# The second product's last part in 128x64 tiles of the array: two matmuls for 64 tokens each in place of one for 128

## The chip, the cores and the metric

The kernel runs on one core of a Trainium2 chip. Its engines are TensorE (PE in the profile, PEld its weight loads), VectorE (DVE), ScalarE (ACT), GpSimd (POOL) and SyncE (SP), which run side by side and wait for each other by semaphores. The metric is device time in microseconds (us) of one execution; the median over several runs counts.

## The reference

Two steps follow each other: an attention with a window of 32 positions and 32 global tokens per batch, and a two-layer product with a gate between the layers. The change lies in the last line.

```python
# attention, B=8 batches, H=8 heads, 512 local + 32 global tokens, head_dim 64
out_g = softmax(scale * q_g @ [k_g, k_l].T) @ [v_g, v_l]
out_l = softmax([scale * q_l @ k_g.T, masked(scale * q_l @ k_l.T)]) @ [v_g, v_l]   # |i - j| <= 32
x = concat(out_g, out_l).transpose(0, 2, 1, 3).reshape(B * S, H * D)                # 4352 x 512
# two products, w_in 512 x 2048, w_out 2048 x 512
h = x @ w_in
g = h * clip(h + 3, 0, 6) / 6
return g @ w_out                                                                    # 4352 x 512
```

## The kernel before

The work is cut by batch. For each of the eight batches the local attention is done in four steps of 128 queries (`local_step`), the 32 global queries in one (`global_steps`), and then the two products are done for the 512 local tokens (`moe_local`). The global tokens of all batches, 8 x 32 = 256, are kept until the end and get their two products there (`moe_global`).

A local step has these matmuls. L741 multiplies 128 queries with the global keys, on the whole 128x128 array. L748 does the window: for each pair of heads and each group of 32 queries a matmul with 64 rows of the array and 32 of its columns, so that eight such 64x32 tiles fit on the array (two halves of rows for two heads, four quarters of columns for four groups of queries). L797 (early batches) turns the probabilities, and L830 (L822 for batch 0) multiplies them with the values. L822 uses slices of 64, 32 and 96 rows of the array beside whole ones. For the global queries L865 computes the scores, again on 64x32 tiles, the first eight matmuls with 32 columns of moving data and the next eight with 512; L904 turns the probabilities and L918 multiplies them with the values.

The products: `first` computes 128 of the 2048 inner columns for 512 tokens (L941, four matmuls that add up over the 512 model columns), ScalarE applies the gate's first half (L948), VectorE the second (L952), and the result goes in half precision to the tile `gs`, with the inner columns on the partitions. `second` computes 128 tokens of the output: 16 matmuls (L964) add up over the 2048 inner columns in one PSUM tile `m`; the weights loaded into the array are 128x128 of `gs` (128 inner columns by 128 tokens) and the moving data are 512 columns of `w_out`. The 16 are issued in four steps of four (`q`). ScalarE or VectorE then copies `m` to `ot` (L410 or L412) and SyncE stores it (L981). For the last 128 tokens of the last batch the output is made in two halves of 256 columns (`halves=2`). There are three tiles `m` and two tiles `gs`.

The order of the work is not written out by hand. Every step is handed to a planner with `add(engine, duration, ...)`, its dependencies, a due time (`key`, shifted by a table of ranks) and the buffers that it takes and gives back. The planner simulates the engines with these durations, sorts all steps by the start that it finds, and the program issues them in that order, each engine its own. Each step of four matmuls in `second` has a duration of 865 ns there and 8 instructions. The ranks move the second products of batches 6 and 7 towards the end: they run from 266.8 us on, among the last attention steps and first products, and the last 112 matmuls of L964, with nothing else between them, end the work of TensorE. At the start, matmuls on a tile of zeros (L1093) keep TensorE busy while the first data come.

Of the kernel before, what the change touches and what calls it, by code (L numbers as in the profile page):

```python
# [175 lines left out]
class Plan:  # L176
# [16 lines left out]
    def add(self, eng, dur, emit, deps=(), key=0.0, acq=None, rel=(), dma=None, cols=0, ins=0):  # L193

        o = Op(eng, dur, emit, deps, key + RANKS.get(self.at, 0.0), acq, rel, 0, dma)
        o.at, o.cols, o.ins = self.at, cols, ins
        o.can = {eng: dur} if isinstance(eng, str) else dict(zip(eng, dur))
        o.n = len(self.ops)
        self.ops.append(o)
        for r in rel:  # L200
            r.held += 1
        return o
# [120 lines left out]
def kernel(  # L323
# [12 lines left out]
    nc = tc.nc  # L336
    P = 128

    B, H, Sl, D = q_l.shape
# [4 lines left out]
    NJ = Sl // P  # L344
    NDFF = dff // P
# [20 lines left out]
    def many(n, shape, dtype, name, pool=sb):  # L366
        return [pool.tile(shape, dtype, tag=f"{name}{i}", name=f"{name}{i}") for i in range(n)]
# [5 lines left out]
    psM = many(3, [P, 512], FP32, "m", pp)  # L373
# [19 lines left out]
    gs = many(2, [P, NDFF, 512], FP16, "gs")  # L393
# [3 lines left out]
    w_out_t = sb.tile([P, NDFF, dm], FP16, tag="wout", name="wout")  # L397
# [10 lines left out]
    def copy(op, out, in_):  # L408
        if op.eng == "ACT":
            nc.scalar.copy(out=out, in_=in_)  # L410
        else:
            nc.vector.tensor_copy(out=out, in_=in_)  # L412
# [521 lines left out]
    def first(c, n, t0, x, xdeps, xrel, set_, key):  # L934

        k = 512 // n

        def pe(op):
            for i in range(k):
                for m in range(NP):  # L940
                    nc.tensor.matmul(out=psM[op.slot][:, i * n:(i + 1) * n],  # L941
                                     lhsT=w_in_t[:, m, (c + i) * P:(c + i + 1) * P],
                                     rhs=x()[:, m, t0:t0 + n], start=(m == 0), stop=(m == NP - 1))
        f = add("PE", 865 + 10 * (k - 1), pe, list(xdeps) + [*wi[c // 4], set_], key=key, acq="M", rel=xrel, cols=2048, ins=2 * k * NP)
        to = add("ACT", 0, lambda op: None, [f], key=key - 2, acq="t1")

        def re(op):
            nc.scalar.activation(out=t1[to.slot], in_=psM[f.slot], func=RELU, bias=0.5, scale=1.0 / 6.0)  # L948
        a = add("ACT", 477, re, [to], key=key - 2)

        def st_(op):
            nc.vector.scalar_tensor_tensor(out=gs[set_.slot][:, c:c + k, t0:t0 + n],  # L952
                                           in0=t1[to.slot].rearrange("f (k t) -> f k t", k=k), scalar=1.0,
                                           in1=psM[f.slot].rearrange("f (k t) -> f k t", k=k),
                                           op0=ALU.min, op1=ALU.mult)
        return add("DVE", 600, st_, [a], key=key - 1, rel=[f, to])

    def second(t0, gdone, set_, dests, keys, halves=1):
        f, n = None, dm // halves
        for a in range(halves):  # L960
            for q in range(4):
                def pe(op, q=q, a=a):
                    for c in range(q * 4, q * 4 + 4):
                        nc.tensor.matmul(out=psM[(f or op).slot][:, a * n:(a + 1) * n], lhsT=gs[set_.slot][:, c, t0:t0 + P],  # L964
                                         rhs=w_out_t[:, c, a * n:(a + 1) * n], start=(c == 0), stop=(c == NDFF - 1))
                deps = gdone[q * 4:q * 4 + 4] + [wo[q * 4]]
                if f is None:
                    f = s = add("PE", 865 / halves, pe, deps, key=keys[q], acq="M", cols=2048 / halves, ins=8)
                else:
                    s = add("PE", 865 / halves, pe, deps + [s], key=keys[q] + 0.01 * a,  # L970
                            rel=[set_] if q == 3 and a == halves - 1 else [], cols=2048 / halves, ins=8)
            if a == 0:
                oo = add("DVE", 0, lambda op: None, [s], key=keys[3] - 1, acq="ot")

            def ev(op, a=a):
                copy(op, ot[oo.slot][:, a * n:(a + 1) * n], psM[f.slot][:, a * n:(a + 1) * n])
            c = add(BOTH, (482 / halves, 603 / halves), ev, [s, oo], key=keys[3] - 1, rel=[f])

            for k, (dst, lo, hi) in enumerate(dests):
                def sto(op, dst=dst, lo=lo, hi=hi, a=a):  # L980
                    nc.sync.dma_start(out=dst[:, a * n:(a + 1) * n], in_=ot[oo.slot][lo:hi, a * n:(a + 1) * n])  # L981
                add("SP", 600, sto, [c], key=keys[3] + 0.001 * (k + 4 * a), rel=[oo],
                    dma=(hi - lo, STORE[0] / halves, STORE[1]))

    def moe_local(b, at, span):
        plan.at = None
        set_ = add("ACT", 0, lambda op: None, xdone[b, 0], key=at - 1, acq="gs")
        parts = PART.get(b, (Sl,))
        left = [0]

        def key():
            left[0] += 1
            return at + span * left[0] / 32
        done = []
        for part, n in enumerate(parts):
            t0, k = sum(parts[:part]), 512 // n
            js = range(t0 // P, (t0 + n) // P)
            now = []
            for c in range(0, NDFF, k):
                plan.at = "first", b, part, c // 4  # L1000
                o = first(c, n, t0, lambda: xt[xt_op[b].slot], [d for j in js for d in xdone[b, j]], [xt_op[b]], set_, key())
                now += [o] * k
            done += [now] * len(js)
        for j in range(NJ):
            row = b * S + G + j * P
            plan.at = "second", b, j
            second(j * P, done[j], set_, [(out[row:row + P, :], 0, P)], [key() for _ in range(4)],
                   2 if b == B - 1 and j == NJ - 1 else 1)

    def moe_global(at, span):  # L1010
        deps = [xgd[b] for b in range(B)]
        plan.at = None
        set_ = add("ACT", 0, lambda op: None, deps, key=at - 1, acq="gs")
        k = 512 // (B * G)
        done = [None] * NDFF
        for c in range(0, NDFF, k):
            plan.at = "first", B, c // 4
            done[c:c + k] = [first(c, B * G, 0, lambda: xg, deps, [], set_, at + span * c / 24)] * k
        rows = out.rearrange("(b s) d -> b s d", s=S)
        per = P // G  # L1020
        for i in range(B // per):
            plan.at = "second", B, i
            second(i * P, done, set_, [(rows[i * per + k, 0:G, :], k * G, (k + 1) * G) for k in range(per)],
                   [at + span * (16 + 4 * i + q) / 24 for q in range(4)])

# [2 lines left out]
    for b in range(B):  # L1030
        if b == 0:
            seq = ["q0", "h", "q1", "k", "v0", "v1", "q2", "v2", "q3", "v3", "v4", "i0", "i1", "i2", "i3", "g"]
            for n, what in enumerate(seq):
                k, i, key = what[0], int(what[1:] or 0), -8.0 + 0.05 * n
# [51 lines left out]
        for j in range(NJ):  # L1086
            xdone[b, j] = local_step(b, j, lead + j)
        xgd[b] = global_steps(b, lead + 3.6)
        moe_local(b, 4.0 * b + 0.5, 4.0)
    moe_global(4.0 * b + 2.5, 1.5)  # L1090

    spare = {"A": [x[:, 0, :] for x in psA], "M": psM, "S": [x[:, 0, :] for x in psS]}
    order = plan.fill(plan.lay(av_last[NEAR, 0]), lambda ring, i: lambda: nc.tensor.matmul(  # L1093
        out=spare[ring][i], lhsT=idle[:, 0:P], rhs=idle))
# [36 lines left out]
```

## Time and profile before

| | us |
|---|---|
| median of 3 runs (lowest to highest) | 330.35 (330.26 to 330.73) |
| the profiled execution, its own time | 330.47 |
| its span in the profile | 328.7 |
| busy: PE, DVE, ACT, POOL | 317.9, 264.4, 249.1, 105.6 |
| L964, 560 matmuls and 560 weight loads: busy | 128.4 and 51.2 |
| L964 from 266 us on: 144 matmuls of 512 columns, 32 of 256 | 33.5 and 4.6 |

Mean durations in the groups by line: a 512-column matmul of L964 379 ns, a 256-column one 273 ns, a weight load 98 ns. The granted clock of TensorE was 0.995 of full speed over the span.

[...] Matmuls follow each other in a pipeline, so that one of 379 ns can start every 216 ns; the distance between the starts, not the duration, says what a matmul costs in a stream. The chain of waits goes back from the last instruction to what released it, step by step; in order of time its rows say where the end was made. In a row of a timeline, the size behind the operation (128*128, 64*32) is the rows and columns of the array that the instruction uses, and the size after it the moving data.

### The profile page before, as it was taken

Reading aid. Unit: us, or ns where it says so; the run is one execution under the profiler, and the core shown is the slowest. Engines: PE = TensorE matmul, PEld = TensorE weight load, DVE = VectorE, ACT = ScalarE, POOL = GpSimd, SP = SyncE. Lnnn points to the kernel's source line nnn. Section 1 sums busy time; section 2 is a strip of 40 time slices with the busy share of each in tenths; the row PEclk is TensorE's granted clock in tenths of the full one; section 3 lists DMA queues with packets and bytes.
Section 4 is the critical chain, followed back from the end, with each engine's and each line's share of the span. In section 5 each row is a group of like instructions: output and inputs, shape, how many; then the busy total and the mean of one; then the engine's idle time right before and its main releaser. Section 6 shows DMA issues by size and latency. Waiting matters only on the chain.

```text
span 328.7 us, 10251 instructions
## 1 busy us (share of the span) xinstructions
PE 317.9 (97%) x3892; PEld 190.7 (58%) x3892; DVE 264.4 (80%) x972; ACT 249.1 (76%) x787; POOL 105.6 (32%) x139
## 2 busy tenths in 40 slices
PE   8799899999999999999899999999999999999996
PEld 4478795678676555645445545554545545448453
DVE  6999999889979999898899799576987997377100
ACT  4789899879968889886888798587977894466121
POOL 8849626962870962137600500041000000000000
PEclk9979999999999999999999999999999999999999
DMA  9999999999999999399999999969753313100032
GB/s 161 174 190 171 197 281 176 159 200 235 194 155 245 178 206 203 47 136 190 205 191 253 165 224 201 198 106 183 185 130 98 35 27 103 59 7 0 3 97 96
DMA packets 152898, 49.83 MB, mean 152 GB/s; under 512 B 137936, under 2 KB 145936, under 8 KB 152848
## 3 DMA queue, kind: packets, MB, share of 16 engines
q0 software_dynamic: 106560, 17.05, 69.9%
q1 hardware_dynamic: 46288, 32.12, 42.5%
q8 instruction: 30, 0.49, 0.6%
q14 instruction: 20, 0.16, 0.1%
HBM read 35.19 MB, written 8.91 MB: 134 GB/s over the span
## 4 chain that ended last, share of the span: by engine, by line
PE 79%; DVE 10%; DMA 5%; ACT 3%; issue 1%; SPq 0%; ACTq 0%
PE m L964 34%; PE m L941 30%; PE a L830 4%; DVE sm L763 3%; DMA et<-pn 2%; PE s L748 2%; DVE gs L952 2%; PE t L797 2%; DMA st<-ve 2%; ACT sm L774 2%; PE a L822 1%; PE t L677 1%; PE s L741 1%; DMA st<-in_q_l_dram 1%; DVE pn L789 1%
## 5 line engine op out<-in xcount | busy, mean ns | idle before, releaser
L964 PE MATMUL m<-wout,gs 128*128 128x512 f16 (+1 forms) x560 | 128.4, 373 | 0.0
L941 PE MATMUL m<-xt,win 128*128 128x512 f16 (+2 forms) x704 | 120.1, 321 | 1.2 <-DVE gs L952 0.7
L774 ACT ACTIVATE sm<-sm,stat 128x128 f32<-128x128 f32 x256 | 100.0, 393 | 13.9 <-DVE stat L763 13.3
L952 DVE SCALAR_TENSOR_TENSOR gs<-t,m 128x512 f16<-128x512 f32 x136 | 91.0, 683 | 14.6 <-ACT t L948 13.9
L941 PEld LDWEIGHTS <-win 128*128 128x128 f16 x768 | 68.3, 98 | 47.9 <-issue 2.8
L948 ACT ACTIVATE t<-m 128x512 f32<-128x512 f32 x136 | 80.1, 594 | 19.8 <-PE m L941 18.9
L964 PEld LDWEIGHTS <-gs 128*128 128x128 f16 x560 | 51.2, 98 | 50.8 <-issue 1.1
L763 DVE CUSTOM_DVE_ANT_0 sm<-s,mask 128x128 f32<-128x128 f32 x256 | 60.0, 283 | 3.9 <-PE s L748 3.4
L774 ACT ACTIVATION_READ_ACCUMULATOR sm<-sm,stat 128x1 f32 x256 | 48.8, 191 | 0.0
L505 POOL DMA_DIRECT2D ve<-in_v_l_dram x40 | 32.7, 828 | 43.3 <-PE a L918 32.4
L789 DVE TENSOR_TENSOR pn<-sm,stat 128x512 f16<-128x512 f32 x64 | 44.0, 688 | 1.1
L410 ACT CAST xt<-a 64x512 f16<-64x512 f32 x55 | 31.7, 577 | 15.9 <-PE a L830 14.1
L505 POOL DMA_DIRECT2D nat<-in_q_l_dram x30 | 27.5, 916 | 30.6 <-PE t L677 15.1
L505 POOL DMA_DIRECT2D nat<-in_k_l_dram x30 | 27.4, 913 | 8.7 <-DMA wout<-in_moe_w_out_dram 5.3
L410 ACT COPY ot<-m 128x512 f32<-128x512 f32 (+1 forms) x21 | 11.8, 562 | 19.3 <-PE m L964 19.1
L763 DVE DVE_READ_ACCUMULATOR2_ANT stat<- 128x1 f32 x256 | 21.0, 82 | 0.0
L830 PEld LDWEIGHTS <-st 128*128 128x128 f16 x448 | 16.6, 98 | 6.4 <-issue 1.8
L830 PE MATMUL a<-et,st 128*128 128x64 f16 x448 | 17.7, 193 | 1.6 <-DMA et<-pn 1.6
L505 POOL DMA_DIRECT2D ve<-in_v_g_dram x8 | 4.9, 608 | 30.3 <-PE a L918 30.3
L785 DVE RECIPROCAL stat<-stat 128x4 f32<-128x4 f32 x64 | 10.9, 172 | 3.5 <-ACT sm L774 2.9
L412 DVE COPY ot<-m 128x512 f32<-128x512 f32 x14 | 9.6, 686 | 5.0 <-PE m L964 5.0
L741 PEld LDWEIGHTS <-qk 128*128 128x128 f16 x224 | 9.4, 96 | 4.9 <-issue 0.4
(86 smaller groups left out, 274.3 us busy)
## 6 DMA issues: line engine op xcount, KB each, us to landing
out_dram<-ot SPq DMA_DIRECT2D x31, 256.0 KB, 3.7
st<-ve SPq DMA_DIRECT2D x14, 384.0 KB, 8.2
nat<-in_q_l_dram POOLq DMA_DIRECT2D x30, 128.0 KB, 6.3
nat<-in_k_l_dram POOLq DMA_DIRECT2D x30, 128.0 KB, 6.5
st<-ve SPq DMA_DIRECT2D x7, 512.0 KB, 8.6
st<-ve SPq DMA_DIRECT2D x14, 256.0 KB, 7.6
ve<-in_v_l_dram POOLq DMA_DIRECT2D x24, 128.0 KB, 5.9
win<-in_moe_w_in_dram POOLq DMA_DIRECT2D x4, 512.0 KB, 9.6
```

The source lines that it names most:

```text
L410: nc.scalar.copy(out=out, in_=in_)
L505: nc.gpsimd.dma_start(out=dst(op), in_=src)
L741: nc.tensor.matmul(out=ps[:, e, p * P:p * P + G], lhsT=lhs, rhs=kgz[r][:, p, e, :])
L763: nc.vector.tensor_tensor_reduce(out=sm[sm_op.slot][:, h, :], in0=psS[s.slot][:, e, p * P:(p + 1) * P], in1=m, scale=-scale, scalar=3.0e38 ...
L774: nc.scalar.activation(out=sm[sm_op.slot][:, h, :], in_=sm[sm_op.slot][:, h, :], func=EXP, scale=-1.0, bias=stat[stat_op.slot][:, 0, h:h + 1],
L785: nc.vector.reciprocal(out=stat[stat_op.slot][:, 2, h0:h1], in_=stat[stat_op.slot][:, 1, h0:h1])
L789: (nc.gpsimd if op.eng == "POOL" else nc.vector).tensor_tensor(out=pn[pn_op.slot][:, h0:h1, :], in0=sm[sm_op.slot][:, h0:h1, :], in1=stat[ ...
L830: nc.tensor.matmul(out=ps[:, p // 2, c0:c0 + 64], lhsT=st[r][:, u * NJ + j, p * P:(p + 1) * P], rhs=et[et_op.slot][:, 2 * p:2 * p + 2, u * ...
L941: nc.tensor.matmul(out=psM[op.slot][:, i * n:(i + 1) * n], lhsT=w_in_t[:, m, (c + i) * P:(c + i + 1) * P], rhs=x()[:, m, t0:t0 + n], start ...
L948: nc.scalar.activation(out=t1[to.slot], in_=psM[f.slot], func=RELU, bias=0.5, scale=1.0 / 6.0)
L952: nc.vector.scalar_tensor_tensor(out=gs[set_.slot][:, c:c + k, t0:t0 + n], in0=t1[to.slot].rearrange("f (k t) -> f k t", k=k), scalar=1.0, ...
L964: nc.tensor.matmul(out=psM[(f or op).slot][:, a * n:(a + 1) * n], lhsT=gs[set_.slot][:, c, t0:t0 + P], rhs=w_out_t[:, c, a * n:(a + 1) * n ...
```

## The change

`second` gets a parameter `rows_`, the number of tokens per matmul. It is 128 as before for batches 0 to 5, and 64 for the last two batches and the global tokens. With 64, each matmul becomes two: one with the weights of tokens 0 to 63 that writes partitions 0 to 63 of `m`, and one with the weights of tokens 64 to 127 that writes partitions 64 to 127. Both use all 128 rows of the array and 64 of its columns, and both take the same moving data. Each matmul has its own weight load, so there are two of these as well. The durations and instruction counts that are handed to the planner stay as they were.

```diff
-    def second(t0, gdone, set_, dests, keys, halves=1):
+    def second(t0, gdone, set_, dests, keys, halves=1, rows_=P):
...
                     for c in range(q * 4, q * 4 + 4):
-                        nc.tensor.matmul(out=psM[(f or op).slot][:, a * n:(a + 1) * n], lhsT=gs[set_.slot][:, c, t0:t0 + P],
-                                         rhs=w_out_t[:, c, a * n:(a + 1) * n], start=(c == 0), stop=(c == NDFF - 1))
+                        for m in range(0, P, rows_):
+                            nc.tensor.matmul(out=psM[(f or op).slot][m:m + rows_, a * n:(a + 1) * n],
+                                             lhsT=gs[set_.slot][:, c, t0 + m:t0 + m + rows_],
+                                             rhs=w_out_t[:, c, a * n:(a + 1) * n], start=(c == 0), stop=(c == NDFF - 1))
...
             second(j * P, done[j], set_, [(out[row:row + P, :], 0, P)], [key() for _ in range(4)],
-                   2 if b == B - 1 and j == NJ - 1 else 1)
+                   2 if b == B - 1 and j == NJ - 1 else 1, P // 2 if b >= B - 2 else P)
...
             second(i * P, done, set_, [(rows[i * per + k, 0:G, :], k * G, (k + 1) * G) for k in range(per)],
-                   [at + span * (16 + 4 * i + q) / 24 for q in range(4)])
+                   [at + span * (16 + 4 * i + q) / 24 for q in range(4)], 1, P // 2)
```

## The prediction

> **What bounds the kernel now.** I read the page's busy times and its chain of waits first, then the chain in order of time for the part where the change acts, then the timeline of TensorE (PE) there.
>
> ```profile
> span 328.7 us, 10251 instructions
> ...
> PE 317.9 (97%) x3892; PEld 190.7 (58%) x3892; DVE 264.4 (80%) x972; ACT 249.1 (76%) x787; POOL 105.6 (32%) x139
> ...
> PE 79%; DVE 10%; DMA 5%; ACT 3%; issue 1%; SPq 0%; ACTq 0%
> PE m L964 34%; PE m L941 30%; PE a L830 4%; DVE sm L763 3%; DMA et<-pn 2%; PE s L748 2%; DVE gs L952 2%; PE t L797 2%; DMA st<-ve 2%; ACT sm L774 2%; PE a L822 1%; PE t L677 1%; PE s L741 1%; DMA st<-in_q_l_dram 1%; DVE pn L789 1%
> ```
>
> PE is busy for 97% of the span, and the chain that ended last runs over it for 79%. L964, the matmul that the change splits, is the largest part of that chain.
>
> Which of L964's matmuls change? Counted in the instruction order that the changed program has, its split matmuls begin right after the L830 group at 266.3 us, and no unsplit one follows. So the change acts from 266.8 us to the end. There the chain, in order of time (start, length, what), is PE almost without a break:
>
> ```profile
> 281.31 1.73 PE m L964 x8
> 283.04 1.73 PE m L941 x8
> 284.76 0.86 PE m L964 x4
> 285.63 19.07 PE m L941 x120
> 304.70 20.77 PE m L964 x112
> 325.47 0.02 issue
> 325.50 0.37 ACT ot L410
> ```
>
> The reader is to see that each entry begins where the one before it ends. The busy times by stretch say the same: PE is busy for 19.60 of the 19.60 us from 266.0 to 285.6 and for 18.90 of 18.90 us up to 304.5, and the list of waits of PE from 266 to 326 us is empty. No cover is left here: a nanosecond added to PE in this part is a nanosecond at the end.
>
> Two prices come from these rows. A 512-column L964 costs 1.73/8 = 0.216 us of stream. The last entry holds 80 of these and 32 of 256 columns: (20.77 - 80 x 0.216)/32 = 0.109 us. Weight loads cost nothing on top: each lasts 98 ns (groups by line) and starts with the matmul ahead of it. L830 shows how little room they need: 16 loads of 128 columns with 64-column matmuls take 0.47 us, 29 ns a pair.
>
> **The change, part by part.** First, what it moves: nothing. The order and the waits of DVE, ACT, POOL and SP are the same in both programs, and PE's order too, with each changed matmul replaced by two. The planner's costs for the step were not altered.
>
> It removes 176 matmuls with 176 weight loads (batch 6: 4 x 16; batch 7: 3 x 16 of 512 columns and 2 x 16 of 256; global tokens: 2 x 16; so 144 and 32) and adds 352 of each, one of a pair writing PSUM partitions 0-63 and the other 64-127.
>
> **Does a pair cost more than the one?** The trace of before has no 128x64 tile. The nearest rows are the 64x32 tiles of L748 and L865 (start, length from first start to last end, array size, tile, count):
>
> ```profile
> 267.65 0.35 PE L741 MATMUL s<-kgz,qk 128*128 128x32 f16 x8
> 267.93 0.36 PE L748 MATMUL s<-qk 64*32 64x96 f16 x32
> 268.23 2.76 PE L964 MATMUL m<-wout,gs 128*128 128x512 f16 x12
> ...
> 270.96 0.37 PE L865 MATMUL s<-qk,gt 64*32 64x512 f16 x1
> ...
> 270.99 0.37 PE L865 MATMUL a<-qk,gt 64*32 64x512 f16 x1
> 271.29 3.63 PE L964 MATMUL m<-wout,gs 128*128 128x512 f16 x16
> ```
>
> L865 is eight matmuls of 512 columns, one on each tile. They start within 0.03 us and each lasts 0.37 us, as one alone does (379 ns for L964): tiles in different columns do run side by side, also into one PSUM bank. L748 goes four times round its eight tiles. Its first and last start are 0.36 - 0.20 = 0.16 us apart (0.20: length of one); read record by record, the rounds follow at 267.985, 268.028 and 268.070, 0.0425 us apart. A single matmul of 96 columns on L964's scale is 0.216 x 96/512 = 0.0405 us plus some 2 ns that every matmul of this trace shows (0.109 is 1 to 2 ns over half of 0.216). So a round of eight costs what one full matmul of that width costs, with the loads of the next round hidden. Carried over, a pair costs 0.216 us, like the one matmul it replaces: **0 us**. The upper bound from these rows is L865's distance between neighbours, 3.5 ns, if every pair paid it: 176 x 0.0035 = 0.6 us. The lower bound is the 2 ns that a matmul costs beyond its columns; were they hidden behind the other tile, 176 x 0.002 = 0.4 us would go. L748 shows them still there, so I take 0.
>
> **Changes of the array's tile size.** Between L741 and L748 the stream breaks. The last of L741's eight starts at 267.827 by its record (0.025 us apart, so the next was due at 267.852), yet L748 starts at 267.93: 0.08 us and more. From L865 to L964 the last tile starts at 270.985, its 512 columns are through 0.216 us later at 271.20, and L964 starts at 271.29: 0.09 us. By single records all such breaks from 260 us on are 90 to 94 ns. Is it the rows or the columns of the tile that count? L822 changes the rows alone:
>
> ```profile
> 29.25 0.28 PE L822 MATMUL a<-et,st 64*128 64x64 f16 x4
> 29.46 0.28 PE L822 MATMUL a<-et,ve 32*128 32x64 f16 x4
> ...
> 29.92 0.28 PE L822 MATMUL a<-et,st 96*128 96x64 f16 x4
> 30.04 0.33 PE L692 MATMUL t<-ident,natg 128*128 128x128 f16 x3
> ```
>
> Four matmuls 0.03 us apart would put the next at 29.37; the one with 32 rows starts at 29.46: 0.09 us again. From 96 to 128 rows there is no break (29.92 + 4 x 0.03 = 30.04). A change of columns alone is not in this trace. Its bounds are 0 (96 to 128 rows) and 96 ns (128 to 64 rows); I take 92 ns, the row of L748 and L865 in the same stretch, in which columns change as well. The Trainium skill's "TensorEngine Tiling (Array Packing)", Tiling Modes, Key Properties, says that changing the tiling mode, and not merely the tile, drains TensorE; it makes no exception for columns, and by it the sum would be the one below.
>
> How many are added? In the changed order the split matmuls stand in nine runs. Their borders with 128-wide work (L830, L741, L904, L918, L941) are 14; the other three borders, with L748 and L865, were changes already. All 14 lie where PE has no idle time: 14 x 0.092 = **+1.29 us**. What the first 64-column loads of a run add behind such a break is not shown either: L748's second round follows its first (267.933 by record) after 0.052 us instead of 0.0425, and L830's 0.029 us holds a whole load. So 0 to 9 x 0.029 = 0.26 us; I take L748's 0.01, 9 x 0.01 = **+0.09 us**.
>
> **Code.** PE has 352 more instructions. Code comes in 30 packets of 16 KB (page, DMA queue q8: 0.49 MB), about one per 7751/30 = 258 of PE's instructions; 1 or 2 more are needed. The last stretch would use 4 instructions in 0.216 us, 14 us to a packet. From 29.75 to 36.69 us two packets followed within 7 us, on busier DMA queues; no stop of PE behind a fetch stands in the late part. Cost 0; uncovered, at most a fetch of 1 to 2 us (the packets' own time).
>
> **Sum.** The profiled execution took 330.47 us (span 328.7, and 1.8 around it); 330.47 + 1.29 + 0.09 = 331.85. The median of the three runs is 0.12 lower, so 331.73. I say 331.7.
>
> **The rivals.**
>
> *Changes of columns are free* (not slower). All 128 rows stay in use, and from 96 to 128 rows the trace shows a change at no cost. Against it: every change to a smaller array in this trace costs 90 ns. Place: the same 14 borders; price 14 x 0 = 0, so 330.4 us, or 330.0 if the 2 ns a pair go too. It decides below 47 ns a border: 14 x 0.047 = 0.66 us is 0.2% of the time, which is about what a measurement of this kernel can tell from no change.
>
> *The weight load of a narrow tile is not hidden.* Each pair would wait for a load before it streams, 176 times: from 0.029 us (all that an L830 load and matmul take) to 0.098 us (a whole load), so 5.1 to 17.2 us more and with the borders 336.9 to 349 us. Against it: L748 hides loads into columns beside running ones. The Trainium skill's "TensorE: Matmul & The Clock Gate", Part 3, The mechanism, states that a weight load overlaps running matmuls only if its row group differs; here all rows are shared, so the rule speaks against the change. The trace disagrees for the full array: L964's loads share all rows with the running matmul and are hidden. The same page's section on LDWEIGHTS gives columns/1.2 ns, by which 64 columns would be an estimated 53 ns and the sum 9.4 us more.
>
> *The two matmuls run one after the other*, so that the change does not do what it says. Then each pair pays twice: 144 x 0.216 + 32 x 0.109 = 34.6 us, with the borders 366 us. For it: 128 rows and 64 columns is a form the trace has never shown, with accumulation on top. Against it: L865.
>
> **How the numbers follow.** Forecast 0.76; free borders 0.10; loads not hidden 0.07; one after the other 0.07. The forecast's own case spans 331.3 to 333.0 (330.47 + 14 x 0.096 + 0.62 + 0.26 = 332.7, and 0.3 for the spread of runs). The range takes in the free borders as well: **330.2 to 333.0**, with 0.14 left out above. Faster by over 0.2% (under 329.7) needs free borders and more: 0.02. Within 0.2% (to 331.0): 0.13, the free borders and a cheap edge of the forecast. Slower: 0.85.
>
> **What would show it.** In the tail behind the last L941 the split pairs should start 0.216 us apart, partners a few ns apart, and the tail should keep its 20.8 us; the first pair should start about 0.09 us later than the old row did. Each of the 14 borders should show a break of 0.09 us. Breaks near 0 mean the first rival; a pair every 0.25 to 0.31 us the second; a matmul every 0.216 us the third. A new idle time of PE ended by DMA or issue in the last 60 us would be the code.

## The result and the profile after

The changed kernel takes 332.13 us in the median of 12 runs (331.0 to 334.54); the kernel before, in 12 runs beside it, 330.59 (329.44 to 331.63). The ratio of the mean times is 1.0055 with a 95% interval of 1.003 to 1.008: slower by 1.8 us, between 1.0 and 2.6; the two medians alone are 1.54 us apart. The forecast was 331.7 us, slower by 1.4.

The profiled execution took 332.91 us. Lines of its page (span; busy times; code packets; the chain by engine):

```profile
span 331.1 us, 10603 instructions
...
PE 321.0 (97%) x4068; PEld 193.8 (59%) x4068; DVE 263.5 (80%) x972; ACT 249.1 (75%) x787; POOL 105.6 (32%) x139
...
q8 instruction: 32, 0.52, 0.7%
...
PE 77%; DVE 10%; DMA 8%; ACT 3%; issue 1%; SPq 0%; ACTq 0%; DVEq 0%
```

There are 176 matmuls and 176 weight loads more, and two packets of code more; PE and its weight loads have 3.1 us more of busy time each, the other engines are within 1 us of what they had. The chain of waits in order of time (start, length, what):

```profile
282.58 0.57 PE a L830 x16
283.16 1.85 PE m L965 x16
285.01 1.83 PE m L941 x8
286.84 0.98 PE m L965 x8
287.82 19.18 PE m L941 x120
307.00 20.90 PE m L965 x224
327.90 0.02 issue
327.93 0.37 ACT ot L410
```

Set these beside the rows of before. The long last entry holds twice as many matmuls and takes 20.90 us instead of 20.77, and a border with its first pair is in that: the pairs are free. The short entries have grown by about 0.1 us each, whichever line they belong to: L830 0.57 (0.47), L965 1.85 (1.73), L941 1.83 (1.73), L965 0.98 (0.86), and the 120 L941 19.18 (19.07). An entry of the chain ends where the next one's instruction begins to count, so a break between two sizes of tile shows up as length of the entry behind it.

A run of four pairs in the timeline (start, length, array size, tile, count):

```profile
267.12 0.63 PE L830 MATMUL a<-et,st 128*128 128x64 f16 x16
267.68 1.05 PE L965 MATMUL m<-wout,gs 128*64 128x512 f16 x8
268.67 0.36 PE L741 MATMUL s<-kgz,qk 128*128 128x32 f16 x8
```

By single records the last L830 starts at 267.559 us and the first pair at 267.682, 0.123 later instead of 0.029: a break of 0.094 us. The next pairs start at 267.922, 268.138 and 268.354, so the first pair takes 0.240 us of the stream and the next ones 0.216; partners start 3 to 4 ns apart. The last partner starts at 268.357 and L741 at 268.669, 0.312 later instead of 0.216: a break of 0.096 us. Here only the columns of the tile change.

The two spans differ by 2.4 us, but not all of that is the change. The unchanged work ahead of it already ends 0.81 us later in this execution: the last L830 entry ahead of the first pair starts at 267.29 us, before at 266.48. From that entry's end to the end of PE's work it is 327.90 - 267.75 = 60.15 us, before 325.47 - 266.95 = 58.52: **1.63 us** belong to the change. The same distance is given below for the runs that keep this order.

### The profile page after: what moved, and what is told of

Same layout as the page of the kernel before. It is cut to its first block, busy times and chain, and to the rows that moved or that the text cites. A ratio compares the mean times of both kernels' runs of the same rounds, so it can differ in the third digit from the quotient of the medians.

```text
span 331.1 us, 10603 instructions
## 1 busy us (share of the span) xinstructions
PE 321.0 (97%) x4068; PEld 193.8 (59%) x4068; DVE 263.5 (80%) x972; ACT 249.1 (75%) x787; POOL 105.6 (32%) x139
## 4 chain that ended last, share of the span: by engine, by line
PE 77%; DVE 10%; DMA 8%; ACT 3%; issue 1%; SPq 0%; ACTq 0%; DVEq 0%
PE m L965 32%; PE m L941 29%; DMA et<-pn 5%; PE a L830 4%; DVE sm L763 3%; PE s L748 2%; DVE gs L952 2%; PE a L822 2%; PE t L797 2%; DMA st<-ve 2%; ACT sm L774 2%; PE t L677 1%; PE s L741 1%; DMA t<-in_k_l_dram 1%; PE t L904 1%
## 5 line engine op out<-in xcount | busy, mean ns | idle before, releaser
L965 PE MATMUL m<-wout,gs 128*128 128x512 f16 (+2 forms) x736 | 128.6, 371 | 0.0
L941 PE MATMUL m<-xt,win 128*128 128x512 f16 (+2 forms) x704 | 120.8, 323 | 0.7 <-DVE gs L952 0.5
L774 ACT ACTIVATE sm<-sm,stat 128x128 f32<-128x128 f32 x256 | 100.0, 393 | 14.1 <-DVE stat L763 13.5
L941 PEld LDWEIGHTS <-win 128*128 128x128 f16 x768 | 68.8, 99 | 47.5 <-issue 3.1
L965 PEld LDWEIGHTS <-gs 128*128 128x128 f16 (+1 forms) x736 | 53.6, 103 | 49.2 <-issue 1.8
L763 DVE CUSTOM_DVE_ANT_0 sm<-s,mask 128x128 f32<-128x128 f32 x256 | 60.0, 284 | 5.2 <-PE s L748 4.7
L774 ACT ACTIVATION_READ_ACCUMULATOR sm<-sm,stat 128x1 f32 x256 | 48.8, 191 | 0.0
L763 DVE DVE_READ_ACCUMULATOR2_ANT stat<- 128x1 f32 x256 | 21.2, 83 | 0.0
L830 PEld LDWEIGHTS <-st 128*128 128x128 f16 x448 | 16.4, 98 | 6.3 <-issue 1.4
L830 PE MATMUL a<-et,st 128*128 128x64 f16 x448 | 17.7, 193 | 1.0 <-DMA et<-pn 1.0
L741 PEld LDWEIGHTS <-qk 128*128 128x128 f16 x224 | 9.3, 96 | 5.1 <-issue 0.8
```

Source lines behind the costliest of these rows:

```text
L741: nc.tensor.matmul(out=ps[:, e, p * P:p * P + G], lhsT=lhs, rhs=kgz[r][:, p, e, :])
L763: nc.vector.tensor_tensor_reduce(out=sm[sm_op.slot][:, h, :], in0=psS[s.slot][:, e, p * P:(p + 1) * P], in1=m, scale=-scale, scalar=3.0e38 ...
L774: nc.scalar.activation(out=sm[sm_op.slot][:, h, :], in_=sm[sm_op.slot][:, h, :], func=EXP, scale=-1.0, bias=stat[stat_op.slot][:, 0, h:h + 1],
L830: nc.tensor.matmul(out=ps[:, p // 2, c0:c0 + 64], lhsT=st[r][:, u * NJ + j, p * P:(p + 1) * P], rhs=et[et_op.slot][:, 2 * p:2 * p + 2, u * ...
L941: nc.tensor.matmul(out=psM[op.slot][:, i * n:(i + 1) * n], lhsT=w_in_t[:, m, (c + i) * P:(c + i + 1) * P], rhs=x()[:, m, t0:t0 + n], start ...
L965: nc.tensor.matmul(out=psM[(f or op).slot][m:m + rows_, a * n:(a + 1) * n], lhsT=gs[set_.slot][:, c, t0 + m:t0 + m + rows_], rhs=w_out_t[: ...
```

## The experiments

The theory from the two traces: the cost sits at the borders, where the array goes from tiles of one size to tiles of another. The rival: it sits in the pairs, in their additional loads and their code. The change has 14 new borders and 176 pairs; the experiments separate the two numbers. "Before" in each ratio is the kernel before, run on the same chip.

### Only the tail split

```diff
-                   2 if b == B - 1 and j == NJ - 1 else 1, P // 2 if b >= B - 2 else P)
+                   2 if b == B - 1 and j == NJ - 1 else 1, P // 2 if b >= B - 1 else P)
```

> Only batch 7 and the global tokens are split: 112 of the 176 pairs, but all of them in the one uninterrupted tail, so 1 new change of the array's tile size instead of 14. Theory (the cost sits at the borders, some 95 ns each, and 20 ns on the first pair behind one): 0.095 + 0.02 = 0.12 us more than before, ratio 1.000. Rival (the cost sits in the pairs, in their extra loads and their code): 112/176 of the change's own cost of about 1.5 to 1.8 us, 1.0 to 1.1 us more, ratio 1.003.

Measured: 330.25 us, ratio 0.9987 (0.9964 to 1.0011). No difference shows, and the rival's 1.003 lies outside the interval. From the end of that L830 entry to the end of PE's work it is 326.18 - 267.53 = 58.65 us in the trace, 0.13 more than before, for the theory's 0.12. The chain of this run, its last entries:

```profile
286.21 19.07 PE m L941 x120
305.29 20.90 PE m L965 x224
```

The tail has the changed kernel's 20.90 us, L941 ahead of it the 19.07 of before: its border with L965 is gone, as batch 6's step there is whole again.

### Only batch 6 split

```diff
-                   2 if b == B - 1 and j == NJ - 1 else 1, P // 2 if b >= B - 2 else P)
+                   2 if b == B - 1 and j == NJ - 1 else 1, P // 2 if b == B - 2 else P)
...
-                   [at + span * (16 + 4 * i + q) / 24 for q in range(4)], 1, P // 2)
+                   [at + span * (16 + 4 * i + q) / 24 for q in range(4)], 1, P)
```

> Only batch 6 is split: 64 of the 176 pairs, which hold 13 of the 14 new changes of the tile size and 8 of the 9 first pairs. Theory (borders): 13 x 0.095 + 8 x 0.02 = 1.4 us more than before, ratio 1.004. Rival (pairs): 64/176 of 1.5 to 1.8 us, 0.6 us more, ratio 1.002.

Measured: 331.81 us, ratio 1.0039 (1.0016 to 1.0063). Theory 1.004, rival 1.002: the value is the theory's, though the interval holds both. The trace decides: from the L830 entry to the end of PE's work it is 327.21 - 267.18 = 60.03 us, 1.51 more than before, where the theory has 1.4 and the rival 0.6. With the run above, a third of the pairs has nearly the whole cost and two thirds have 0.13 us of it. The tail has its old length:

```profile
287.25 19.18 PE m L941 x120
306.43 20.77 PE m L965 x112
```

### Borders without more pairs

In the tail every second matmul of a sum is split, the others are whole.

```diff
                     for c in range(q * 4, q * 4 + 4):
-                        for m in range(0, P, rows_):
+                        w_ = rows_ if c % 2 == 0 else P
+                        for m in range(0, P, w_):
...
-                   2 if b == B - 1 and j == NJ - 1 else 1, P // 2 if b >= B - 2 else P)
+                   2 if b == B - 1 and j == NJ - 1 else 1, P // 2 if b >= B - 1 else P)
```

with `w_` for `rows_` in the matmul.

> In the tail (batch 7 and the global tokens) every second matmul of a sum is split and the others are left whole: 56 pairs, half as many as the tail can hold, and 112 new changes of the tile size, one at each matmul. Theory (borders): 112 x 0.095 + 56 x 0.02 = 11.8 us more than before, ratio 1.036. Rival (pairs): 56/176 of 1.5 to 1.8 us, 0.5 us more, ratio 1.002.

Measured: 342.72 us, ratio 1.036 (1.0329 to 1.0391), the theory's number; the rival falls. Half of the tail's pairs cost 12 us because each now stands between two borders. The tail in the chain:

```profile
304.20 33.50 PE m L966 x168
```

33.50 - 20.77 = 12.73 us for 112 borders, 0.114 us each. By single records 0.094 and 0.096 us of this are the breaks into and out of the narrow tiles; the rest is a first pair that needs 0.024 us more than a pair in a stream, a first whole matmul that needs 0.010 us more, and the 0.003 us between partners.

### All batches split

```diff
-                   2 if b == B - 1 and j == NJ - 1 else 1, P // 2 if b >= B - 2 else P)
+                   2 if b == B - 1 and j == NJ - 1 else 1, P // 2)
```

> All batches are split: 560 pairs and 109 new changes of the tile size, 66 of them into a run of pairs. Theory (borders): 109 x 0.095 + 66 x 0.02 = 11.7 us more than before if TensorE had no idle time anywhere; up to a few us less where it waits in the earlier batches; ratio 1.025 to 1.036. Rival (pairs): 560/176 of 1.5 to 1.8 us, 4.8 to 5.7 us more, ratio 1.015 to 1.017.

Measured: 344.08 us, ratio 1.0385 (1.0343 to 1.0428): 12.7 us more, far above the rival's 1.017 and a little above the theory's 1.036, which the interval holds. Two things that the theory left out stand in the trace. The first is a wait. The waits of PE from 40 to 280 us (who, for what: us in total, times, longest):

```profile
PE s L748 <- issue: 2.0, 1, 2.0
```

Before has no such entry there. "issue" means that nothing shown held the instruction back. The records point to late code. The page has 35 packets of code instead of 30, and 3892 matmuls and as many loads in 30 packets before make some 260 of PE's instructions to a packet. The stop lasts from 105.75 to 107.73 us, and a packet of code lands within it, at 106.20. By the records 3265 of PE's instructions (matmuls, loads and its few semaphore instructions) lie ahead of it, and the two long stops on issue of the last run below have 4 x 256 and 10 x 256 more ahead. No run changes the code alone, so this remains an argument from the records.

The second is the clock behind that stop (busy times by stretch; the column behind POOL is the granted clock):

```profile
109.14:112.56 3.42, 3.42 (x33) 1.83 (x29) 1.49 (x9) 2.23 (x8) 0.00 (x0) 0.50 0.23 55
```

At full speed the work of these 3.42 us would have taken half of it, so 1.7 us went there. The theory's 11.7, the 2.0 and the 1.7, less the wait of 1.6 us for `et` that before has and this run has not, make 13.8 us; the spans of the two profiled executions differ by 342.3 - 328.7 = 13.6.

### Four tiles instead of two

```diff
-... P // 2 if b >= B - 2 else P)
+... P // 4 if b >= B - 2 else P)
...
-... for q in range(4)], 1, P // 2)
+... for q in range(4)], 1, P // 4)
```

> The same matmuls as in the change are split in four for 32 tokens each (128x32 tiles) instead of in two: 704 matmuls in place of 176, the same places of the borders. Theory (side by side, cost at the borders alone): as the changed kernel within 0.3 us, 1.4 to 1.8 us more than before, ratio 1.004 to 1.006; in the trace four matmuls within some 10 ns of each other every 0.216 us. Rival (each load or each instruction of a pair costs): the extra over before doubles or triples, 3 to 5 us more, ratio 1.009 to 1.015.

Measured: 332.34 us, ratio 1.0058 (1.0032 to 1.0085), as the change itself. The tail, now 448 matmuls with 448 loads:

```profile
305.22 20.90 PE m L965 x448
```

It takes 20.77 us with 112 matmuls and 20.90 with 224 or 448, where the difference is one border with its first round: the columns of the array are shared without loss. The rival's 1.009 lies outside the interval, too.

### The order of the pairs

The two loops of the change are exchanged: four matmuls on the first tile, then four on the second.

```diff
-                    for c in range(q * 4, q * 4 + 4):
-                        for m in range(0, P, rows_):
+                    for m in range(0, P, rows_):
+                        for c in range(q * 4, q * 4 + 4):
```

> The change with the two loops exchanged: four matmuls on the first tile, then four on the second, the same matmuls in another order. Theory (TensorE starts matmuls in order, so two tiles overlap only where neighbours in the order lie on different tiles): a step of four pairs takes 6 distances of 0.216 us instead of 4 where steps follow each other and 7 at the end of a run, so 36 x 2 x 0.216 + 8 x 2 x 0.109 + 9 x 0.216 = 19.2 us more than the changed kernel, 20.7 us more than before, ratio 1.063. Rival (each tile works off its own matmuls independently of the order): as the changed kernel, ratio 1.005.

Measured: 332.44 us, ratio 1.0062 (1.0029 to 1.0094). My theory of this run is refuted: the order cost 0.2 us at most (60.34 us from the L830 entry to the end of PE's work, 60.15 with the pairs side by side). The tail in the chain is

```profile
307.53 20.93 PE m L965 x224
```

and the single records of the first step (start in us, length in ns) show how:

```
268.048 403   268.062 403
268.288 379   268.302 379
268.504 379   268.518 379
268.720 379   268.733 379
```

Two streams run side by side, 14 ns apart. Three matmuls for the first tile stand in the program ahead of the second tile's first, yet that one starts 14 ns after the very first: it has overtaken them. The Trainium skill's "TensorE: Matmul & The Clock Gate", Part 3, The mechanism, states that matmuls start strictly in program order; this trace does not agree. The records do not name the tile; that these eight take four distances of 0.216 us is what shows two tiles at work.

### How far a matmul can overtake

All 32 matmuls of a sum are issued at its last step (`q == 3`): first 16 on one tile and then 16 on the other, and, in a second kernel, the same with the pairs side by side.

```diff
-                    for c in range(q * 4, q * 4 + 4):
-                        for m in range(0, P, rows_):
+                    for m in range(0, P, rows_):
+                        for c in range(q * 4, q * 4 + 4) if rows_ == P else range(NDFF) if q == 3 else ():
```

The second kernel has the same new `range` for `c`, with the two loops in their old order.

> As the change, but the 32 matmuls of a sum are issued together at its last step, first all 16 on one tile, then all 16 on the other, so that a matmul and its partner stand 32 instructions apart instead of 2 (8 when the loops are exchanged). Gathering also leaves 6 new changes of the tile size instead of 14. Theory (a matmul may start ahead of others that wait for another tile, and reaches past 32 instructions): 6 x 0.095 + 0.1 = 0.7 us more than before, ratio 1.002. Rival (it reaches some 8 to 16 instructions only, or not at all): a sum takes 30 distances of 0.216 us instead of 16, for 9 sums of 512 columns, and half of that for 2 of 256, 27.2 + 3.0 = 30 us more, ratio about 1.09; a reach in between gives a time in between.

> As the change, pairs side by side, but all 16 pairs of a sum are issued together at its last step. All 176 pairs are there, with 6 new changes of the tile size instead of 14. Theory (the cost sits at the borders): 6 x 0.095 + 5 x 0.02 = 0.7 us more than before, ratio 1.002. Rival (the cost sits in the pairs): 1.5 to 1.8 us more, as the changed kernel, ratio 1.005.

Measured: tile after tile 359.37 us, ratio 1.0856 (1.0813 to 1.0898); side by side 338.6 us, ratio 1.0241 (1.0211 to 1.0272). Both theories missed. That the first comes near its rival's 1.09 is partly chance: some 5 us of its loss are waits that come with the gathering, as the second shows, and not with the order.

The first: one sum and the tail in the chain of the run tile after tile,

```profile
270.07 6.19 PE m L965 x32
...
320.09 32.10 PE m L965 x214
```

and side by side:

```profile
271.09 3.57 PE m L965 x32
...
312.33 20.90 PE m L965 x224
```

(Ten records of the 224 are missing in the first trace.) A sum takes 6.19/0.216, some 28 distances, instead of 16. In the single records of that sum the second tile's first matmul starts at 272.622 us, 7 ns after the thirteenth of the first tile (272.615); so it overtook the three that were left and no more. That agrees with the run before this one, where exactly three had to be overtaken. The other three sums that stand alone take the same 6.2 us, and in the tail each group of 16 starts beside the last four of the group ahead. Four sums that stand alone cost 2.6 us each and the tail 11.2, 21.7 us together. The two kernels differ by only 359.37 - 338.6 = 20.8, since in the other one a sum that stands alone ran at a low clock, 1.7 us longer (below).

The second: with 6 new borders, 0.7 us were expected and 7.7 were found (336.4 - 328.7, the spans of the profiled executions). The waits of PE from 255 us on name most of it:

```profile
PE s L865 <- DVE stat L763: 3.2, 1, 3.2
PE a L918 <- DVE eg L412: 0.9, 1, 0.9
PE a L830 <- DVE xg L927: 0.8, 1, 0.8
```

In the kernel before and after the change this list is empty. The small steps of batch 6 had filled PE's time while the softmax ran (L763 is its maximum); gathered, they come too late for that; this is read from the order, not tested by itself. And a stretch behind the idle time ran at half speed (busy times by stretch; the column behind POOL is the granted clock):

```profile
278.00:282.40 4.40, 2.76 (x53) 1.81 (x47) 1.67 (x4) 0.00 (x0) 0.00 (x0) 1.00 0.16 61
282.40:286.10 3.70, 3.70 (x23) 1.61 (x22) 0.00 (x0) 1.16 (x2) 0.00 (x0) 0.54 0.02 4
```

PE was busy for 2.76 of 4.40 us, and then the clock stood at 0.54 for 3.7 us; at full speed these would have taken about 2.0, so 1.7 us went there. The waits, 4.9, the clock, 1.7, and the borders, 0.7, make 7.3 of the 7.7 us. The clock's part does not follow from the idle time alone: the run tile after tile has the same three waits, and there the clock stayed at full speed:

```profile
282.00:290.00 8.00, 6.36 (x68) 3.76 (x66) 1.67 (x4) 1.16 (x2) 0.00 (x0) 1.00 0.09 35
```

So this kernel does not price the borders, but it shows what the small steps were worth where they stood.

### More work on the small tiles

In the kernel before, L741's products for batches 1 to 7 are made on the 64x32 tiles of L748.

```diff
-                for e in range(2):
+                for e in range(2) if near else ():
...
-                    else:
-                        nc.tensor.matmul(out=ps[:, e, p * P:p * P + G], lhsT=lhs, rhs=kgz[r][:, p, e, :])
+            for p in () if near else range(NP):
+                for u in range(NU):
+                    for e in range(2):
+                        rows, q0 = slice(e * D, (e + 1) * D), UQ + j * P + u * UQ
+                        nc.tensor.matmul(out=ps[u * UQ:(u + 1) * UQ, e, p * P:p * P + G],
+                                         lhsT=qk[r][rows, 0, p, q0:q0 + UQ], rhs=kgz[r][rows, p, e, :])
```

> The kernel before, with the products of the queries and the global keys (L741, eight matmuls on the whole array) of batches 1 to 7 made on the 64x32 tiles of L748 just ahead of it: the border moves ahead of them and none is added. Theory (matmuls on eight tiles cost one distance a round, and no border is added): eight distances of 0.025 us give way to four rounds of eight starts at 3.5 ns, 0.11 us, so 28 x 0.09 = 2.5 us less if TensorE is the bound throughout, 1 to 2.5 us less with its idle times, ratio 0.992 to 0.997. Rival (rounds of so few columns wait for their weight loads, and 1344 more instructions are to be fetched): 0 to 2 us more, ratio 1.000 to 1.006.

Measured: 345.06 us, ratio 1.0425 (1.0373 to 1.0478): slower by far more than either said. One step in the timeline (start, length, line), and PE's longest wait of the run:

```profile
149.04 0.30 PE L744 MATMUL s<-kgz,qk 64*32 64x32 f16 x32
149.25 0.47 PE L752 MATMUL s<-qk 64*32 64x96 f16 x32
149.65 0.39 PE L968 MATMUL m<-wout,gs 128*128 128x512 f16 x1
```

```profile
PE s L752 <- issue: 4.7, 3, 2.7
```

L752 is L748's old work. Its 32 matmuls lasted 0.36 us before and last 0.47 here, since they start every 8.3 ns by single records, and the first starts 0.089 us after the last of L744 (149.160 to 149.249), although the size of the tile stays the same. It looks as if instructions come no faster behind a burst of 32 short ones; the run does not show the reason. A step takes 149.65 - 148.94 = 0.71 us (148.94: when the matmul ahead of it is through) instead of 154.00 - 153.42 = 0.58 before, so 28 x 0.13 = 3.6 us.

The waits on issue are 4.7 us, nearly all of it in two stops, 134.24 to 135.97 us and 186.28 to 189.02. A packet of code lands within each, at 134.49 and 187.77, and 4289 and 5825 of PE's instructions lie ahead. With the 3265 of the run on all batches these are multiples of 256 apart, about a packet's worth each time, which points to late code.

The same list of waits has 2.3 us of L968 for ScalarE's L778 and 2.0 us of L834 for VectorE's L767 (the softmax's L774 and L763 of before), which before has not. The granted clock stood at 0.50 for 3.4 us twice, behind the second of these waits and at the last stop on issue, about 3 us of loss. These terms, 3.6, 4.7, 4.3 and 3, come to more than the 14.1 us between the spans; before has 1.6 us of waiting for `et`, of which 0.5 is left here. What brought the waits for the softmax is not shown.

## Why the prediction was right

- **What bounds**: right. PE's list of waits from 266 us on is empty after the change too, and what the breaks add up to there, 1.62 us, came out at the end as 1.63.
- **A pair costs nothing**: right. The bound from below (the 2 ns per matmul) and that from above (3.5 ns per pair) are both out: 112 pairs changed the tail by 0.13 us, and its one border with its first pair explains 0.12 of it.
- **Borders, 14 x 0.092**: right. A change of columns alone, which the trace of before did not have, costs what one of rows does: 7 breaks of 0.093 to 0.094 and 7 of 0.096 us, 1.33 us for the forecast's 1.29. One reading was loose: by the distances the break from L741 to L748 is 0.081 us (0.106 less 0.025), not 0.090 to 0.094 like the others.
- **First pair of a run**: mis-sized. 0.01 us was taken from L748, whose loads are 32 columns wide; with 64 it is 0.024 (9 x 0.024 = 0.22 us for 0.09), and with 32 columns in the run on four tiles the second round was 0.011 us late, as in L748.
- **Left out**: the first whole matmul behind a run also starts its stream 0.010 us late, 7 x 0.010 = 0.07 us. Together 1.33 + 0.22 + 0.07 = 1.62, against 1.63 read from the chain. Two smaller terms nearly cancel: the 0.003 us between partners at the end of each of the nine runs, and the 0.010 that the two whole matmuls behind L748 and L865 paid before.
- **Code**: 0, right at this dose: two more packets, no wait. In the run with all batches split a wait of 2.0 us appears, and the records point to late code there.
- **The rivals**: free borders fall by the breaks; loads that are not hidden and matmuls one after the other fall by the pairs' distance of 0.216 us. The rival about the loads named the Trainium skill's rule on row groups ("TensorE: Matmul & The Clock Gate", Part 3, The mechanism). The trace after does not agree with it either: the loads into 64 columns last 110 ns and vanish behind matmuls on the same rows.
- **The size**: 1.38 forecast, 1.62 by the trace, 1.8 (1.0 to 2.6) by the means of the measured times and 1.54 by their medians. Between these the runs do not decide.

## What to carry to other kernels

Splitting a matmul over columns of the array neither gains nor costs in a stream with 256 or 512 columns of moving data, where weight loads are hidden anyway (32 columns on eight tiles were another matter); what it costs is each change between tile sizes in PE's order, about 0.11 us with its first matmul, where PE is the bound. So count the borders in the order that the scheduler makes, not the matmuls in the loop, and put work of one tile size together, unless the small steps between are what fills PE's waits. Count the added instructions, too: where 1120 and 1344 more were spread over the kernel, PE stopped for 2.0 and 4.7 us, by the records for code; 1056 more at its end (four tiles) brought no stop. Here only the tail could be split for nothing, and for nothing in return.

## What was not expected of the hardware

- A matmul on a free tile overtakes waiting matmuls of another tile, three of them and not more (a step of four on each tile lost next to nothing; sixteen took 28 distances instead of 16 where a sum stood alone).
- Behind 32 short matmuls on small tiles in a row, the next 32 started every 8.3 ns instead of about 5, and 0.089 us late.
- A stop of 2.0 us (all batches split) and stops of 1.6 us within 4.4 (pairs gathered) were followed by 3.4 us at a granted clock of 0.50. The same stops in the run tile after tile were not, nor was the one of 3.2 us ahead of them. The idle time alone does not tell when the clock falls.
- PE stopped on issue for 2.0, 1.7 and 2.7 us in two runs, at places that are multiples of 256 of its instructions apart, and each time a packet of code landed within the stop.
